# Shifting every stationary operand of the rounded products by 64 bytes, and two small moves in the turn to the output steps

## The chip, the cores and the metric

The kernel runs on one core of one Trainium2 chip. The metric is the device time of one execution in microseconds (us), the median of three runs. The engines are PE (TensorE, with its weight loads listed apart as PEld), DVE (VectorE), ACT (ScalarE), POOL (GpSimd) and SP (SyncE, which here only issues DMAs).

## The reference, cut to what matters

Three networks follow each other: a windowed attention over 4 x 8 heads of 576 positions, a gated product network, and a second network with a SiLU between its two products.

```
attn = softmax(mask(q @ k.T * scale)) @ v      # window of 64 behind each position
x  = attn as 2304 x 512
x  = ((x @ w1) * (x @ w2)) @ w3 @ w_out        # 512 -> 1024 -> 1024 -> 512
h  = x @ w_in                                  # 512 -> 2048
y  = (h * sigmoid(h)) @ w_out2                 # 2048 -> 512
```

All inputs come as 64-bit floats' words, which the kernel converts itself.

## The kernel before, in words

**Rounded products.** Most matmuls take operands that were split into a high part (rounded to the type `fp32r`) and a low part (what the rounding left). A product of two such operands is three matmuls: high by high, high by low, low by high (`PASSES`). Each matmul has a stationary operand (128 x 128, loaded by a weight load of its own) and a moving one, which streams past it: 384 columns in the first two stages, 256 in the last.

**Stages.** `phase_w` converts weights and forms w3 @ w_out (plain products) while the first attention units run. `phase_a(blk, hooks)` runs six times, once for each block of 384 positions: 16 groups `ab` of 12 matmuls (stationary `hl`, the split w1 and w2; moving `xa` and `xb`; L693 and one left-over at L698) and 4 groups `x` of 24 (stationary `wp`, moving `p` and `q`; L723 and L729). Blocks 0 to 4 carry the attention between their groups: `unit` calls `halves_to`, and each `half` puts scores `s`, values `o` and three transposes `t` on PE, and the softmax on DVE and ACT. The transposes (L428) read `sm`, the normalised weights that DVE writes last in a unit (L418). Chunks of w_in are converted in the same units. The last block has no attention. Then come 12 steps `d` of the hidden layer (`h_slot`, `product`, L1019: 7 groups of 12, stationary `wi`, moving the tiles `xop`, which lie in the slots x0 to x6), and 36 output steps `m` (`out_products`, L1170: 42 matmuls of 256 columns, stationary `hi`, `lo` and `a`, moving the weight parts `wo`). Both use a fast matrix scheme of seven products, so there are sums of operands to build.

**Order.** Everything runs under a manual schedule: what stands in the program is the order on each engine, and an engine does its instructions in that order. Ahead of output step m stand, for its operands, `f_load` (a DMA of hidden values), `f_sums` (DVE), `f_high` (ACT casts) and `f_low` (DVE subtractions); for its weights, `o_load` and `o_part` (ACT casts and DVE subtractions for pair n of w_out2; step m with m % 4 = e uses the pairs 2e and 2e + 1). `keep` stores a hidden tile, `read` empties a PSUM bank.

**Where operands lie.** Tiles live in named slots that are used again and again; `SLOTS` gives sizes in 4-byte elements, 1024 where a name is missing. In the program as built, every slot but x0 to x6 begins 128 bytes behind a multiple of 256. The slots x0 to x5 have 1568 elements, that is 6272 bytes or 24.5 times 256, so they begin by turns 128 and 0 bytes behind such a multiple. All operands of rounded products thus begin at a multiple of 128 bytes, except the ones that `shifted` cuts out: `hi` and `lo` in x0 to x5 begin 16 elements, 64 bytes, further. Of the 42 stationary operands of an output step that leaves 36 shifted and 6 (`a`) not; in every fourth step (m % 4 = 3: `lo` in xa, `hi` in x6) all 42 are unshifted. Over 36 steps 972 of 1512 are shifted and 27 x 6 + 9 x 42 = 540 are not.

Of the kernel before, what the change touches and what calls it, by code (L numbers as in the profile page):

```python
# [9 lines left out]
F32 = mybir.dt.float32  # L10
F32R = mybir.dt.float32r
# [31 lines left out]
def tile_window_attention_ffn(ctx, tc, qkv, qkp, vp, w1, w2, w3t, w_out, w_in, w_out2, out):  # L43
# [53 lines left out]
    x2d = dram.tile([4, 128, T], F32, name="x2d", tag="x2d")  # L97
    w_in32 = dram.tile([4, 128, FF2], F32, name="w_in32", tag="w_in32")

    SLOTS = {"p": 4096, "q": 2304, "xa": 1536, "xb": 1536, "xr": 1536, "st": 1024, "x2": 4096, "cv_r": 512, "cv_b": 512}  # L100
    SLOTS.update({"xe": 2304, **{f"x{i}": 1568 if i < 6 else 1536 for i in range(7)}})

    def slot(name, tag, dims, dtype=F32, pool=None, bufs=1):

        t = (pool or main).tile([128, SLOTS.get(tag, 1024)], dtype, name=name, tag=tag, bufs=bufs)
        n = int(np.prod(dims))
        letters = "abcd"[: len(dims)]
        sizes = {x: d for x, d in zip(letters[1:], dims[1:])}
        return t[:, :n].rearrange(f"p ({' '.join(letters)}) -> p {' '.join(letters)}", **sizes)
# [636 lines left out]
                nc.gpsimd.memset(f32(pt[i, 0][hs, 1 - h]), 0.0)  # L746

    with tc.manual_schedule():
        xr = slot("xr", "xr", [4, NB])
        xe = slot("xe", "xe", [2304])  # L750
        phase_w()
# [30 lines left out]
        late.close()  # L782

        end = ctx.enter_context(tc.tile_pool(name="end", bufs=1, side="right"))
        PAIRS = FF2 // 256
        SUPER = T // (2 * NB)
        DUOS = PAIRS // 2
        NDUO = DUOS * SUPER
# [4 lines left out]
        gd = dram.tile([SUPER, DUOS, 128, 4, 768], F32, name="gd", tag="gd")  # L793
        t32 = dram.tile([PAIRS, 128, 7, 256], F32, name="t32", tag="t32")
        xop, raw, wop, oop = {}, {}, {}, {}
        g, bank, tmp = {}, {}, {}
# [8 lines left out]
        def sub(eng, out, a, b):  # L805
            tt(eng, out, a, b, ALU.subtract)
# [13 lines left out]
        shared = {}  # L820

        def unit_tile(kind, n, i):

            tag = UNITS[n // 2][6 if i == 3 else 3 * (n % 2) + i]
            key = kind, tag
            if key not in shared:
                if tag[0] == "p":
                    if (kind, "p") not in shared:
                        shared[kind, "p"] = slot(f"{kind}_p", "p", [4, 1024], F32R)
                    shared[key] = shared[kind, "p"][:, int(tag[1])]  # L830
                else:
                    shared[key] = slot(f"{kind}_{tag}", tag, [1024], F32R)
            return shared[key]
# [95 lines left out]
        def o_load(n):  # L929
            if n in (0, 2, 4):  # L930
                t = [tmp["q"][:, 0:1024], tmp["q"][:, 1024:1536], tmp["q"][:, 1536:1792]]
            elif n == 1:
                t = [xe[:, 0:1024], xe[:, 1024:1536], xe[:, 1536:1792]]
            elif n == 7:
                x = slot("or7", "xb", [1536])
                t = [x[:, 0:1024], x[:, 1024:1536], st[3][:, 768:1024]]
            else:
                t = [st[2], st[3][:, 0:512], st[3][:, 512:768]]
            raw["o", n] = t
            for x, y in zip(t, (slice(0, 4), slice(4, 6), slice(6, 7))):  # L940
                nc.sync.dma_start(out=x, in_=t32[n, :, y].rearrange("p a n -> p (a n)"))
# [13 lines left out]
        def o_part(n, part):  # L955
            if part == 0:
                o_tiles(n)
            r0, r1, r2 = raw["o", n]
            src = [r0[:, 0:512], r0[:, 512:1024], r1, r2]
            src = [x.rearrange("p (a n) -> p a n", n=256) for x in src]  # L960
            for i in ((0, 1), (2,), (3,), ())[part]:
                nc.scalar.copy(out=oop[n][i][0], in_=src[i])
            for i in ((), (0,), (1,), (2, 3))[part]:
                sub(nc.vector, oop[n][i][1], src[i], f32(oop[n][i][0]))
# [43 lines left out]
        def product(d, k):  # L1008
            t, first, i = WHERE[k]
            j, e = divmod(d, DUOS)  # L1010
            x, name = xop[j, i], home(d, k)
            fresh = k in (0, 2, 5)
            if fresh:
                bank[name] = pso.tile([128, 2, 512], F32, name=f"{name}{d}_{k}", tag=name)
            for q in range(2):
                w = wop[2 * e + q][t]
                for kt in range(2):
                    for n, (l, r) in enumerate(PASSES):
                        nc.tensor.matmul(  # L1019
                            bank[name][:, q, 0:NB], lhsT=w[:, l, first + kt], rhs=x[:, kt, r, :],  # L1020
                            start=(fresh and kt == 0 and n == 0), stop=(kt == 1 and n == 2), skip_group_check=True,
                        )
# [7 lines left out]
        def keep(d, op, t):  # L1030
            j, e = divmod(d, DUOS)
            nc.sync.dma_start(out=gd[j, e, :, op], in_=t.rearrange("p t q n -> p (t q n)"))
# [47 lines left out]
        def f_load(m):  # L1080
            if m >= NTG * DUOS:
                return
            if m == 0 or m % 3 == 2:
                t = xe[:, 0:1024], xe[:, 1024:2048]
            elif m > 1 and m % 3 == 1:
                t = slot(f"f{m}", "w21", [1024]), slot(f"fs{m}", "w22", [1024])
            else:
                t = tmp["q"][:, 0:1024], tmp["q"][:, 1024:2048]
            raw["f", m] = t
            tg, e = divmod(m, DUOS)  # L1090
            cols = slice(tg % 3 * 256, tg % 3 * 256 + 256)
            nc.sync.dma_start(out=t[0].rearrange("p (a n) -> p a n", a=4), in_=gd[tg // 3, e, :, :, cols])

        def f_sums(m):

            if m < NTG * DUOS:
                f, t = [x.rearrange("p (a n) -> p a n", a=4) for x in raw["f", m]]
                add(nc.vector, t[:, 0], f[:, 3], f[:, 2])  # L1100
                sub(nc.vector, t[:, 1], f[:, 3], f[:, 0])
                sub(nc.vector, t[:, 2], t[:, 0], f[:, 0])
                sub(nc.vector, t[:, 3], f[:, 1], t[:, 2])

        def shifted(name, tag):

            t = slot(name, tag, [SLOTS[tag]], F32R, end)
            t = t[:, 16:1552] if SLOTS[tag] > 1536 else t
            return t.rearrange("p (a n) -> p a n", a=6)

        def f_high(m):
            if m < NTG * DUOS:
                n = m % 4
                if n == 3:
                    lo = slot(f"lo{m}", "xa", [6, 256], F32R)
                    a = unit_tile("wo", 6, 3)[:, 0:512]
                else:
                    if "a11" not in tmp:
                        tmp["a11"] = slot("a11", "xr", [3, 512], F32R)
                    lo = shifted(f"lo{m}", ("x1", "x5", "x4")[n])  # L1120
                    a = tmp["a11"][:, n]
                hi = shifted(f"hi{m}", ("x0", "x2", "x3", "x6")[n])
                a = [a[:, 0:256], a[:, 256:512]]
                sets[m] = lo, hi, a
                f, t = raw["f", m]
                for i, x in ((0, f), (3, t)):
                    nc.scalar.copy(out=hi[:, i : i + 3], in_=x[:, 0:768].rearrange("p (a n) -> p a n", a=3))  # L1127
                nc.scalar.copy(out=a[0], in_=t[:, 768:1024])

        def f_low(m):  # L1130
            if m < NTG * DUOS:
                lo, hi, a = sets[m]
                f, t = raw["f", m]
                for i, x in ((0, f), (3, t)):
                    sub(nc.vector, lo[:, i : i + 3], x[:, 0:768].rearrange("p (a n) -> p a n", a=3), f32(hi[:, i : i + 3]))
                sub(nc.vector, a[1], t[:, 768:1024], f32(a[0]))
# [121 lines left out]
        for j in range(1, SUPER):  # L1258
# [6 lines left out]
            for k, x in ((14, 3), (16, 4), (18, 6)):  # L1265
                at(s + k, x_op, j, x)
        PLAN = tuple((n, 12 + 5 * n) for n in range(PAIRS))
        FIRST_OUT = 7 * DUOS * (SUPER - 1)
# [20 lines left out]
        xb, xa = slot("gxb", "xb", [2, 768]), slot("gxa", "xa", [2, 768])  # L1289
        st = [slot(f"gst{i}", "st", [1024], bufs=4) for i in range(4)]  # L1290
# [15 lines left out]
        o_part(5, 3)  # L1306
        o_load(6)
        keep(last, 2, g["a22"])
        f_sums(2)
        product(last, 4)  # L1310
        product(last, 6)
        read(last, 4)
        f_sums(3)
        for part in range(4):
            o_part(6, part)
        keep(last, 1, g["a12"])
        o_load(7)
        f_high(2)
        read(last, 6)
        keep(last, 3, g["two", last % 2])  # L1320
        f_low(2)
        f_load(5)
        for part in range(4):
            o_part(7, part)
        f_high(3)
        f_low(3)
        f_load(6)
        f_sums(4)
# [85 lines left out]
```

## Time and profile before

| | |
|---|---|
| median of 3 runs | 822.27 us (822.09 to 823.5) |
| the profiled execution | 821.25 us, of which the span of its instructions is 819.3 us |
| busy in the span | PE 804.2, DVE 633.0, ACT 562.8, POOL 340.2 us |
| stretch 112 to 166 us (blocks 0 and 1) | PE 54.00 of 54.00, DVE 39.37, ACT 44.02 |
| stretch 166 to 397 us (blocks 1 to 4) | PE 230.37 of 231.00, DVE 197.96, ACT 204.58 |
| stretch 460.77 to 642.44 us (hidden steps) | PE 181.21 of 181.67, DMA share 0.74 |
| stretch 642.44 to 819.30 us (output steps) | PE 171.44 of 176.86, DMA share 0.43 |

PE looks busy nearly throughout, but a matmul's own record is longer than the distance to the next one, since they are pipelined. How fast PE goes is read from starts: so many matmuls from one start to another. The profiled execution is 1.02 us under the median.

### The profile page before, as it was taken

The numbers are of one execution on the slowest core, as the hardware profiler recorded it, in microseconds if no ns is written. First come the engines' busy times: TensorE is split into PE (matmuls) and PEld (weight loads), VectorE is DVE, ScalarE is ACT, GpSimd is POOL, SyncE is SP. The second block draws the span as 40 slices with busy tenths as digits, with TensorE's granted clock in tenths as the row PEclk, the third lists the DMA queues.
The fourth block names the chain that finished last, engine by engine and source line by source line (L and its number), as shares of the span: only waits on it lengthen the run. The fifth ranks groups of instructions, "written<-read, shape, count | busy, mean of one in ns | idle before, by whom it ended". The sixth has DMA issues, their size and how long they took to land.

```text
span 819.3 us, 15577 instructions
## 1 busy us (share of the span) xinstructions
PE 804.2 (98%) x5066; PEld 760.5 (93%) x5066; DVE 633.0 (77%) x1549; ACT 562.8 (69%) x1314; POOL 340.2 (42%) x422
## 2 busy tenths in 40 slices
PE   8899999999999999999999999999999999999998
PEld 4455799999999999999999999999999899999998
DVE  7878867788888988988747568858546899988882
ACT  6889878889899888989735567765657654334440
POOL 5768576667677677776733204443000000000000
PEclk9999999999999999999999999999999999999999
DMA  9998323534544544544232449797685745544421
GB/s 301 344 310 269 107 76 116 178 101 147 174 136 160 178 145 135 177 150 135 87 126 77 161 165 321 265 352 294 221 290 179 259 154 156 154 139 146 129 78 52
DMA packets 79791, 146.33 MB, mean 179 GB/s; under 512 B 7136, under 2 KB 46432, under 8 KB 79712
## 3 DMA queue, kind: packets, MB, share of 16 engines
q1 hardware_dynamic: 76112, 140.50, 51.7%
q10 hardware_dynamic: 3600, 4.85, 1.6%
q8 instruction: 40, 0.66, 0.3%
q14 instruction: 39, 0.32, 0.1%
HBM read 105.48 MB, written 39.85 MB: 177 GB/s over the span
## 4 chain that ended last, share of the span: by engine, by line
PE 72%; POOL 6%; ACT 6%; issue 4%; DVE 2%; DMA 2%; SPq 0%; ACTq 0%; POOLq 0%; DVEq 0%
PE ab L693 16%; PE oa L1170 11%; PE x L723 9%; PE ob L1170 8%; PE ha L1019 6%; PE hd L1019 6%; PE hb L1019 5%; PE hc L1019 3%; PE accw L614 2%; POOL klo L351 2%; PE t L428 2%; POOL vhl L369 1%; POOL p L117 1%; POOL xr L474 1%; PE o L462 1%
## 5 line engine op out<-in xcount | busy, mean ns | idle before, releaser
L693 PE MATMUL ab<-xa,hl 128*128 128x384 f32 x576 | 118.9, 341 | 0.0
L693 PE MATMUL ab<-xb,hl 128*128 128x384 f32 x570 | 115.2, 334 | 0.0
L693 PEld LDWEIGHTS ab<-xb,hl 128*128 128x128 f32 x570 | 100.3, 188 | 0.0
L693 PEld LDWEIGHTS ab<-xa,hl 128*128 128x128 f32 x576 | 99.1, 188 | 0.0
L1170 PE MATMUL oa<-wo_w,hi 128*128 128x256 f32 x408 | 74.3, 277 | 0.0
L351 POOL TENSOR_TENSOR klo<-qk,qkhi 64x192 fp32r<-64x192 f32 x110 | 67.2, 611 | 8.4 <-ACT qkhi L345 2.3
L723 PE MATMUL x<-p,wp 128*128 128x384 f32 x360 | 69.0, 339 | 0.0
L474 POOL TENSOR_TENSOR xr<-ot 128x128 f32<-128x128 f32 x55 | 32.7, 595 | 72.8 <-DVE ot L473 56.0
L1170 PEld LDWEIGHTS oa<-wo_w,hi 128*128 128x128 f32 x408 | 61.8, 188 | 0.0
L723 PEld LDWEIGHTS x<-p,wp 128*128 128x128 f32 x360 | 61.8, 188 | 0.0
L1170 PE MATMUL oa<-wo_w,lo 128*128 128x256 f32 x204 | 56.7, 278 | 0.0
L1019 PE MATMUL ha<-xop,wi_w 128*128 128x384 f32 x288 | 54.4, 337 | 0.5 <-ACT gxb L1041 0.5
L1019 PEld LDWEIGHTS ha<-xop,wi_w 128*128 128x128 f32 x288 | 50.5, 188 | 1.1 <-ACT gxb L1041 1.1
L406 ACT ACTIVATE sm<-sm,nm 128x192 f32<-128x192 f32 x110 | 49.3, 449 | 1.4
L887 POOL TENSOR_TENSOR cv_b<-cv_b,cv_r 128x512 int32<-128x512 int32 x16 | 22.3, 1394 | 62.7 <-DVE cv_b L884 50.9
L1019 PE MATMUL hd<-xop,wi_w 128*128 128x384 f32 x252 | 48.0, 336 | 0.0
L345 ACT CAST qkhi<-qk 128x768 fp32r<-128x768 f32 x55 | 46.0, 836 | 1.2
L392 DVE CUSTOM_DVE_ANT_0 sm<-s,consts 128x192 f32<-128x192 f32 x144 | 45.2, 352 | 1.3 <-PE s L385 0.9
L1019 PEld LDWEIGHTS hd<-xop,wi_w 128*128 128x128 f32 x252 | 44.4, 188 | 0.0
L428 PE MATMUL t<-consts,sm 128*128 128x128 f32 x216 | 35.9, 275 | 7.4 <-DVE sm L418 5.3
L1170 PE MATMUL ob<-wo_w,hi 128*128 128x256 f32 x216 | 40.8, 278 | 0.3 <-ACT hi L1127 0.3
L723 PE MATMUL x<-q,wp 128*128 128x384 f32 x210 | 40.3, 334 | 0.0
(279 smaller groups left out, 2261.1 us busy)
## 6 DMA issues: line engine op xcount, KB each, us to landing
qk<-in_qkv SPq DMA_DIRECT2D x55, 384.0 KB, 3.1
words<-in_w3t SPq DMA_DIRECT2D x16, 512.0 KB, 6.5
words<-in_w SPq DMA_DIRECT2D x16, 512.0 KB, 6.2
xe<-in_w_in SPq DMA_DIRECT2D x16, 512.0 KB, 4.6
gq<-in_w_out SPq DMA_DIRECT2D x16, 512.0 KB, 4.9
gd<-gxa SPq DMA_DIRECT2D x18, 384.0 KB, 4.4
gd<-gst SPq DMA_DIRECT2D x18, 384.0 KB, 4.9
xe<-gd SPq DMA_DIRECT2D x13, 512.0 KB, 4.0
```

Of the source, the lines that this page charges most:

```text
L345: nc.scalar.copy(out=hi, in_=t)
L351: nc.gpsimd.tensor_tensor(out=k_lo[g % 2][hs, h * 192 : h * 192 + 192], in0=t[hs, n], in1=f32(hi[hs, n]), op=ALU.subtract)
L392: nc.vector.tensor_tensor_reduce(out=sm[g % 2][:, h, :], in0=s_ps[:, h, :], in1=consts[:, at + 64 - 64 * h : at + 256 - 64 * h], op0=ALU.a ...
L406: nc.scalar.activation(out=e[:, h, :], in_=x, func=AF.Exp, scale=-1.0, bias=nm[:, h : h + 1], accum_out=sums_of[g % 2][:, h, 0:1])
L428: nc.tensor.transpose(t_ps[:, i * 128 : i * 128 + 128], x[:, at : at + 128], id_sb)
L474: nc.gpsimd.tensor_tensor(out=xr[:, c, r : r + 128], in0=t[:, 0:128], in1=t[:, 128:256], op=ALU.add)
L614: nc.tensor.matmul(acc[i], lhsT=w3x[s % 7][:, i * 128 : (i + 1) * 128], rhs=wo[:, j], start=(j == 0), stop=(j == 7))
L693: nc.tensor.matmul(acc, lhsT=w[:, l, fs], rhs=x[k // 2][:, k % 2, r, :], start=(k == 0 and n == 0), stop=(k == 3 and n == 2),)
L723: nc.tensor.matmul(acc, lhsT=wp[f][:, l, o * 128 : (o + 1) * 128], rhs=p[f][:, r, :], start=(f == 0 and n == 0), stop=(f == 7 and n == 2),)
L887: nc.gpsimd.tensor_tensor(out=c.b, in0=c.b, in1=c.r, op=ALU.add)
L1019: nc.tensor.matmul(bank[name][:, q, 0:NB], lhsT=w[:, l, first + kt], rhs=x[:, kt, r, :], start=(fresh and kt == 0 and n == 0), stop=(kt == ...
L1170: nc.tensor.matmul(dst, lhsT=lhs[l], rhs=rhs[r], start=(first and e == 0 and q == 0 and n == 0), stop=(e == DUOS - 1 and q == 1 and n == 2 ...
```

## The change

The sizes of slots and the order in which they are first asked for change, so that slots which hold stationary operands begin 64 bytes behind a multiple of 128; `SKIP` and the argument `skip` move a tile inside its slot by 16 elements. `xa` and the `xop` tiles, which are moving operands, get skips that leave them at a multiple of 128. The moving weight parts `wo` of the output steps share their slots with stationary ones and are shifted with them.

In the program as built, all stationary operands of the lines L693, L698, L723, L729, L1019 and L1170 (two to six lines further down in the new file) begin 64 or 192 bytes behind a multiple of 256. Moving operands of the first five of these lines begin 0 or 128 behind one, as before. Of the 1512 products of the output steps, whose moving operands all began 128 behind one, 1323 now have a moving operand at 192 and 189 one at 64; stationary and moving lie 0 apart modulo 256 in 999 of them and 128 apart in 513. Before, they lay 64 apart (either way) in 972 and 0 apart in 540. In the hidden steps they lay 0 apart in 576 products and 128 apart in 432; now they lie 64 apart, either way, in all 1008. Operands of the attention and of `phase_w` stay where they were modulo 128.

The second part moves steps ahead of the output: `f_high(2)` and `f_low(2)` go ahead of `o_part(6)`, `f_high(3)` too, `o_load(7)` goes up.

```diff
-    SLOTS = {"p": 4096, "q": 2304, "xa": 1536, "xb": 1536, "xr": 1536, "st": 1024, "x2": 4096, "cv_r": 512, "cv_b": 512}
-    SLOTS.update({"xe": 2304, **{f"x{i}": 1568 if i < 6 else 1536 for i in range(7)}})
+    SLOTS = {"p": 4112, "q": 2304, "xa": 1552, "xb": 1536, "xr": 1552, "st": 1024, "x2": 4096, "cv_r": 512, "cv_b": 512}
+    SLOTS.update({"xe": 2304, **{f"x{i}": 1552 for i in range(7)}})
+    SKIP = {"xa": 16, "x6": 16, "x1": 16, "x3": 16, "x5": 16}
...
+        t = t[:, SKIP.get(tag, 0) if skip is None else skip :]
...
     with tc.manual_schedule():
+        for t in ("q", "xb", "p", *[f"w{i}" for i in range(24)], "xa"):
+            slot(f"first_{t}", t, [1])
...
         end = ctx.enter_context(tc.tile_pool(name="end", bufs=1, side="right"))
+        for i in (6, 0, 1, 2, 3, 4, 5):
+            slot(f"first_x{i}", f"x{i}", [1], pool=end)
...
-                        shared[kind, "p"] = slot(f"{kind}_p", "p", [4, 1024], F32R)
+                        shared[kind, "p"] = slot(f"{kind}_p", "p", [4, 1024], F32R, skip=16)
...
         def shifted(name, tag):
 
-            t = slot(name, tag, [SLOTS[tag]], F32R, end)
-            t = t[:, 16:1552] if SLOTS[tag] > 1536 else t
-            return t.rearrange("p (a n) -> p a n", a=6)
+            return slot(name, tag, [6, 256], F32R, None if tag == "xa" else end, skip=16 - SKIP.get(tag, 0))
...
-                    lo = slot(f"lo{m}", "xa", [6, 256], F32R)
+                    lo = shifted(f"lo{m}", "xa")
...
-                        tmp["a11"] = slot("a11", "xr", [3, 512], F32R)
+                        tmp["a11"] = slot("a11", "xr", [3, 512], F32R, skip=16)
...
         keep(last, 2, g["a22"])
+        o_load(7)
         f_sums(2)
+        f_high(2)
         product(last, 4)
         product(last, 6)
         read(last, 4)
         f_sums(3)
-        for part in range(4):
-            o_part(6, part)
+        f_low(2)
+        f_load(5)
         keep(last, 1, g["a12"])
-        o_load(7)
-        f_high(2)
         read(last, 6)
         keep(last, 3, g["two", last % 2])
-        f_low(2)
-        f_load(5)
-        for part in range(4):
-            o_part(7, part)
         f_high(3)
+        for n in (6, 7):
+            for part in range(4):
+                o_part(n, part)
         f_low(3)
```

On DVE, at the turn from the hidden to the output steps, this stood before. `xe` and `gq` are the sums for steps 2 and 3, `wo_w<-gst` is `o_part(6)`, `wo_p<-or` and the row behind it `o_part(7)`, `gxa<-hd` is `read(last, 6)`, `lo<-xe` is `f_low(2)` and `lo<-gq` `f_low(3)`.

```order
L800 TENSOR_TENSOR gq<-gq 128x256 x4
L800 TENSOR_TENSOR wo_w_7839<-gst_6122,wo_w_7839 128x512
L800 TENSOR_TENSOR wo_w_7840<-gst_6122,wo_w_7840 128x512
L800 TENSOR_TENSOR wo_w_7841<-gst_6123,wo_w_7841 128x512
L800 TENSOR_TENSOR wo_w_7702<-gst_6123,wo_w_7702 128x256
L800 TENSOR_TENSOR gxa<-hd_5_7705,gxa 128x768
L800 TENSOR_TENSOR lo_7855<-xe,hi_7856 128x768 x2
L800 TENSOR_TENSOR a_7673<-xe,a_7673 128x256
L800 TENSOR_TENSOR wo_p<-or_7851,wo_p 128x512 x3
```

The same place of DVE in the new program:

```order
L806 TENSOR_TENSOR gq<-gq 128x256 x4
L806 TENSOR_TENSOR lo_7849<-xe,hi_7850 128x768 x2
L806 TENSOR_TENSOR a_7708<-xe,a_7708 128x256
L806 TENSOR_TENSOR gxa<-hd_5_7740,gxa 128x768
L806 TENSOR_TENSOR wo_w_7897<-gst_6157,wo_w_7897 128x512
L806 TENSOR_TENSOR wo_w_7898<-gst_6157,wo_w_7898 128x512
L806 TENSOR_TENSOR wo_w_7899<-gst_6158,wo_w_7899 128x512
L806 TENSOR_TENSOR wo_w_7737<-gst_6158,wo_w_7737 128x256
L806 TENSOR_TENSOR wo_p<-or_7841,wo_p 128x512 x3
```

The low parts for step 2 now stand ahead of `read(last, 6)`, and the four subtractions of `o_part(6)` behind both.

On ACT, the same place before (`gst<-hb` is `read(last, 4)`, `gxa<-gxa` the SiLU of `read(last, 6)`):

```order
L1028 ACTIVATE gst_6120<-hb_0_7609 128x768
L962 CAST wo_w_7839<-gst_6122 128x512
L962 CAST wo_w_7840<-gst_6122 128x512
L962 CAST wo_w_7841<-gst_6123 128x512
L962 CAST wo_w_7702<-gst_6123 128x256
L1127 CAST hi_7856<-xe 128x768 x2
L1128 CAST a_7673<-xe 128x256
L1028 ACTIVATE gxa<-gxa 128x768
L962 CAST wo_p<-or_7851 128x512 x3
L962 CAST wo_p<-gst_6123 128x256
L1127 CAST hi_7877<-gq 128x768 x2
```

And in the new program:

```order
L1131 CAST hi_7850<-xe 128x768 x2
L1132 CAST a_7708<-xe 128x256
L1034 ACTIVATE gst_6155<-hb_0_7644 128x768
L1034 ACTIVATE gxa<-gxa 128x768
L1131 CAST hi_7893<-gq 128x768 x2
L1132 CAST wo_p<-gq 128x256
L968 CAST wo_w_7897<-gst_6157 128x512
L968 CAST wo_w_7898<-gst_6157 128x512
L968 CAST wo_w_7899<-gst_6158 128x512
L968 CAST wo_w_7737<-gst_6158 128x256
L968 CAST wo_p<-or_7841 128x512 x3
```

The casts of `o_part(6)` now stand behind the SiLU `gxa<-gxa`, which needs DVE's `gxa<-hd`, and behind the casts of `f_high(3)`. On SP the load of pair 7 and the load for step 5 moved ahead of the stores of the last hidden tiles; PE and POOL keep their order.

## Rows read from the trace of the kernel before

**Rows 1.** The page: busy time of the engines, and PE's granted clock in 40 slices.

```profile
PE 804.2 (98%) x5066; PEld 760.5 (93%) x5066; DVE 633.0 (77%) x1549; ACT 562.8 (69%) x1314; POOL 340.2 (42%) x422
...
PEclk9999999999999999999999999999999999999999
```

**Rows 2.** Chain that ended last, output steps: start us, us, what (matmuls).

```profile
728.60 2.72 PE oa L1170 x24
...
733.44 2.88 PE oa L1170 x24
```

**Rows 3.** The chain, block 5 of the gated network.

```profile
414.50 29.64 PE ab L693 x171
...
449.33 11.44 PE x L723 x66
```

**Rows 4.** The chain, a hidden step: a group with moving slot x4, one with x1.

```profile
547.70 2.08 PE hb L1019 x12
549.78 2.12 PE ha L1019 x12
```

**Rows 5.** Timeline of PE in block 1, transposes of five units: start us, us, what.

```profile
174.45 0.49 PE L428 MATMUL t<-consts,sm 128*128 128x128 f32 x3
...
195.42 0.49 PE L428 MATMUL t<-consts,sm 128*128 128x128 f32 x3
```

**Rows 6.** Timeline of DVE in block 1, the instructions on which those transposes wait.

```profile
172.31 0.56 DVE L418 TENSOR_TENSOR sm<-sm,rs 128x384 f32<-128x384 f32 x1
...
193.66 0.56 DVE L418 TENSOR_TENSOR sm<-sm,rs 128x384 f32<-128x384 f32 x1
```

**Rows 7.** Timeline of all engines, one attention unit late in block 4.

```profile
379.91 0.56 DVE L418 TENSOR_TENSOR sm<-sm,rs 128x384 f32<-128x384 f32 x1
...
380.61 0.52 PE L428 MATMUL t<-consts,sm 128*128 128x128 f32 x3
380.85 0.42 DVE L472 TENSOR_TENSOR ot<-o,ot 64x256 f32<-64x256 f32 x1 [0.38 <-ACT ot L471]
...
382.69 0.51 ACT L114 CAST q<-a 128x384 fp32r<-128x384 f32 x1 [0.83 <-DVE a L709]
...
384.85 0.48 ACT L707 COPY a<-ab 128x384 f32<-128x384 f32 x1
...
386.19 0.42 DVE L472 TENSOR_TENSOR ot<-o,ot 64x256 f32<-64x256 f32 x1 [0.38 <-ACT ot L471]
```

**Rows 8.** Waits from 140 to 167 us: who for whom, us, times, longest.

```profile
ACT pt L438 <- PE t L428: 1.2, 3, 0.6
```

**Rows 9.** The chain, two places in the hidden steps.

```profile
490.36 2.38 PE ha L1019 x12
...
527.07 4.74 DMA gd<-gxb
```

**Rows 10.** Timeline of all engines at the turn to output step 2.

```profile
645.00 1.97 ACT L962 CAST wo_w<-gst 128x512 fp32r<-128x512 f32 x4 [3.59 <-DMA gst<-t]
645.66 2.23 DVE L800 TENSOR_TENSOR wo_w<-gst,wo_w 128x512 fp32r<-128x512 f32 x4 [3.19 <-ACT wo_w L962]
...
646.88 1.56 ACT L1127 CAST hi<-xe 128x768 fp32r<-128x768 f32 x2
...
647.76 0.50 PE L1170 MATMUL ob<-wo_w,hi 128*128 128x256 f32 x2 [0.33 <-ACT hi L1127]
647.81 0.95 DVE L800 TENSOR_TENSOR gxa<-hd,gxa 128x768 f32<-128x768 f32 x1
648.67 1.82 DVE L800 TENSOR_TENSOR lo<-xe,hi 128x768 fp32r<-128x768 f32 x2
648.79 0.84 ACT L1028 ACTIVATE gxa<-gxa 128x768 f32<-128x768 f32 x1
...
649.68 0.38 PE L1170 MATMUL ob<-wo_w,lo 128*128 128x256 f32 x1 [1.42 <-DVE lo L800]
...
653.21 0.95 DVE L800 TENSOR_TENSOR lo<-gq,hi 128x768 fp32r<-128x768 f32 x1
```

More of the change, by code (lines that the diff above doesn't have):

```diff
@@ L98, in tile_window_attention_ffn, with slot @@
     w_in32 = dram.tile([4, 128, FF2], F32, name="w_in32", tag="w_in32")
-    SLOTS = {"p": 4096, "q": 2304, "xa": 1536, "xb": 1536, "xr": 1536, "st": 1024, "x2": 4096, "cv_r": 512, "cv_b": 512}
-    SLOTS.update({"xe": 2304, **{f"x{i}": 1568 if i < 6 else 1536 for i in range(7)}})
-    def slot(name, tag, dims, dtype=F32, pool=None, bufs=1):
+    SLOTS = {"p": 4112, "q": 2304, "xa": 1552, "xb": 1536, "xr": 1552, "st": 1024, "x2": 4096, "cv_r": 512, "cv_b": 512}
+    SLOTS.update({"xe": 2304, **{f"x{i}": 1552 for i in range(7)}})
+    SKIP = {"xa": 16, "x6": 16, "x1": 16, "x3": 16, "x5": 16}
+    def slot(name, tag, dims, dtype=F32, pool=None, bufs=1, skip=None):
         t = (pool or main).tile([128, SLOTS.get(tag, 1024)], dtype, name=name, tag=tag, bufs=bufs)
         n = int(np.prod(dims))
+        t = t[:, SKIP.get(tag, 0) if skip is None else skip :]
         letters = "abcd"[: len(dims)]
```

## Prediction

> **What bounds the kernel now.** I read the page first: PE is busy for 98% of the span at the full clock, 2.4 GHz, in every slice [rows 1]. But overlapping records hide the question, so I took the distance from one matmul's start to the next from the chain.
>
> In the output steps 24 matmuls of 256 columns take 2.72 us where the stationary operands are shifted, 113.3 ns each, and 2.88 us, 120.0 ns each, in a step where none is [rows 2]. The columns alone are 256 / 2.4 = 106.7 ns, so 6.7 or 13.3 ns come on top. With 384 columns and nothing shifted, 171 matmuls take 29.64 us and 66 take 11.44: 173.3 ns, which is 160 and again 13.3 [rows 3]. The extra is the same at both lengths, so I expect a shifted operand to save the same 6.7 ns at 384 columns.
>
> A second reading: in the hidden steps a group of 12 takes 2.08 us with the moving slot x4 and 2.12 with x1, that is 3.3 ns more per matmul, with stationary operands that lie alike [rows 4]. What differs is where the moving operand lies: modulo 256 at the same place as the stationary one, or 128 bytes away. So the price is not the stationary address's alone; the place of the two to each other counts.
>
> Then I asked where PE is the bound. In block 1 the transposes come every 5.24 us (20.97 over four) and the DVE instruction that feeds them every 5.34 (21.35 over four); its result is ready 1.58 us early at 174.45 and 1.20 at 195.42 [rows 5, 6]. DVE falls back by 0.1 us per unit, although PE does not hold it. Late in block 4 the reserve is gone: the result is ready at 380.47 and the transposes start 0.14 later [rows 7]. The same rows show why DVE goes at 5.34: a ring without PE. DVE's L472 to L709 run back to back, ACT's L114 waits for L709, ACT then works through to L707 and the copies behind it, and for these the next L472 waits: 380.85 to 386.19. From about 166 to 397 us the attention is paced by this ring.
>
> **The change part by part.** The sum is against the profiled execution's 821.25 us; the runs' median is 1.02 above.
>
> A, blocks 0 and 1 up to 166 us. Some 250 rounded products, 6.7 ns each: 1.7 us at most. ACT and DVE still wait for PE here, ACT 1.2 us for transposes [rows 8], so a faster PE moves the ring forward by about that. Bounds 0 and -1.7; I take **-1.2**, the wait that the row shows.
>
> From there to 397 us: 0. The 1,000 or so products get faster, and PE waits at each transposition instead, by 5.34 less 5.08 us a unit (24 x 6.7 ns off 5.24) [rows 5, 6].
>
> B, 397 to 460.8 us, the last 73 products of block 4 and the 288 of block 5, without a ring: 361 x 6.7 = **-2.4**. Bound 0, if 384 columns gain nothing.
>
> C, hidden steps: 1008 x 6.7 = -6.7; where the moving slot lies 128 away, 432 products also lose their 3.3 ns, -1.4, if a distance of 64 frees them of it. I count half, -0.7. Against that stand waits that PE's speed uncovers: the group at 490.36 already takes 2.38 us instead of 2.12, for ACT, and the store of gxb, 4.74 us, sits on the chain ahead of another [rows 9]. DMAs and ACT do not get faster, so I add 0.9 for these two and their kind (each grows by 0.3 us over the four groups between). **-6.5**, bounds -8.1 and -4 (and 0 without a gain at 384 columns).
>
> D, output steps. Two prices are possible, and this is the largest uncertain term. If only the stationary address counts, the 540 unshifted products fall from 120.0 to 113.3 ns [rows 2]: -3.6. If the place to each other counts, the shared slots undo the gain: stationary and moving are now both shifted, 0 or 128 apart, and no product is 64 apart any more. The 972 that were go from 113.3 to 120.0: +6.5; and 513 lie 128 apart and pay up to 3.3 more [rows 4], +1.7, of which I count half. No row shows a shifted moving operand. I take the second, **+7.4**, because x1 against x4 shows the relation at work; the bounds are -3.6 and +8.2.
>
> E, the turn. Step 2 waits 0.33 us for its casts and 1.42 for its low parts, because DVE does `o_part(6)` first, after idling 3.19 us for it [rows 10]. The move fills that idle time: low parts from 642.5 to 644.7 (1.82, and some 0.35 for `a`), then `read(last, 6)` to 645.5. Both waits go. But ACT's casts for pair 6 now stand behind the SiLU, which follows that DVE sum (0.84, to 646.4), and behind the casts for step 3 (1.56 and some 0.3, to 648.3); then come 1.97 for pair 6 and as much for pair 7, to 652.2. DVE's subtractions end 0.9 behind a set of casts, as they did before, at 653.1, and only then come step 3's low parts: 653.21 before, so all but unchanged, the first half at 654.05. Step 3 needs them at its third matmul. So what is late next is step 3, which starts about 653.9 instead of 654.7: **-0.8**. Bounds 0 and -1.75. SP's moved load for pair 7 is hidden: it was not waited for longer than pair 6's casts last.
>
> Shifting tiles inside slots costs the other engines nothing that a row shows, and the empty first allocations issue nothing.
>
> Sum: -1.2 - 2.4 - 6.5 + 7.4 - 0.8 = -3.5, so 817.75 on the profiled execution's scale, **818.8 us** at the median.
>
> The Trainium skill, in "TensorE: Matmul & The Clock Gate" (sections "Wait — 56ns, not 53.3ns?" and "Step-by-step: what each phase is for"), speaks against any gain: starts are N / 2.4 plus about 2.5 ns apart, and weight loads have a read port of their own and take nothing from a running matmul. By that, 256 columns would cost 109.2 ns wherever operands lie, and the sum would be E alone. This trace disagrees: 113.3 and 120.0.
>
> **The rivals.**
> - *Both addresses count* (above): 818.8, by itself 816 to 821.2. Chance 0.48.
> - *The stationary address alone counts.* For it: both the shifted forms in the output steps cost the same, and the moving ones all lay alike there. Against: x1 and x4. D is -3.6: 821.25 - 14.5 + 1.02 = 807.8, between 805 and 811. Chance 0.27.
> - *Slower.* The extra at 384 columns has another origin than at 256 (there the load has 53 ns more to hide in), A to C are nothing, and D turns to +7.4: 821.25 + 6.6 + 1.02 = 828.9. It decides from a gain under 6.6 us / 1619 products (A to C) = 4.1 ns each. Against it: the same 13.3 at both lengths. Chance 0.11.
> - *No address effect*, as by the cited rule: the shifts do nothing, E remains, 821.5. Against: 120.0 beside 113.3. Chance 0.05.
> - *The attention follows PE.* If the ring had play that the rows don't show, some 1,000 more products count, 7 us: 811.8 with the first case. Against: PE waits already. Chance 0.04.
> - The rest, 0.05: no gain at 384 columns but one in the output steps, 817.9, or waits in the hidden steps that eat C.
>
> **How the numbers follow.** Between 805 and 822 lie nearly all of the first two cases and the last three; the slow one is left out: 0.8. A measurement tells from no change what is beyond 0.2%, 820.6 to 823.9. Faster: 0.41 of the first case, 0.27, 0.04 and 0.04 of the rest, 0.76. Same: 0.06 of the first, 0.05 of the fourth, 0.11. Slower: the third and what is left of the first and the rest, 0.13.
>
> **What would show it.** In the profile after: twelve matmuls of 384 columns in 2.00 us instead of 2.08, with no difference between slots, if the gain carries over. In the output steps 24 matmuls in 2.88 us throughout by the first case, 2.72 throughout by the second. Transposes in blocks 1 to 4 still 5.34 us apart, with PE waiting for L418. Step 2 without a wait, step 3 with about a microsecond of it. The prediction fails by 11 us if shifted moving operands cost nothing, and by 10 the other way if 384 columns gain nothing.

## The result and the profile after

The changed kernel takes 831.33 us (median of 4 runs, 830.93 to 832.43), the kernel before 822.18 in the same measurement: ratio 1.0117, 95% interval 1.01 to 1.0134. It is 9.1 us slower. The forecast was 818.8, with a range from 805 to 822.

The page of the changed kernel: busy times, and PE's granted clock in 40 slices (against [rows 1]).

```profile
PE 811.7 (98%) x5066; PEld 768.5 (93%) x5066; DVE 633.6 (76%) x1549; ACT 561.9 (68%) x1314; POOL 340.5 (41%) x422
...
PEclk9999999999999999999999999999999899999999
```

One slice is no longer at full clock, the 33rd, around 660 us. That is the turn.

The chain that ended last in the changed kernel, at the places of [rows 2 to 4] and at the turn: start, length, what.

```profile
415.41 24.70 PE ab L695 x142
...
450.39 10.65 PE x L725 x61
...
546.86 2.08 PE ha L1025 x12
...
551.02 2.10 PE ha L1025 x12
...
650.05 7.46 DMA gd<-gxa
657.51 0.02 issue
657.54 0.97 DVE lo L806
658.51 0.04 issue
658.55 1.22 PE ob L1174 x4
...
691.19 2.85 PE oa L1174 x24
```

With 384 columns nothing was gained: 24.70 / 142 = 173.9 ns and 10.65 / 61 = 174.6, where [rows 3] gave 173.3. Twelve hidden products take 2.08 and 2.10 us, not 2.00. In the output steps 24 products take 2.85 us, 118.8 ns each, where [rows 2] had 2.72 and 2.88. And the output is reached through the landing of a store, of which [rows 10] show nothing.

Both programs issue the same 5066 matmuls in the same order, so their starts can be compared one by one. The changed kernel is behind by 0.6 us when block 0 ends, by 0.7 at the end of block 4, 1.1 at the end of block 5, 1.05 at the end of the hidden steps (642.44 us in the kernel before). Over the next 120 matmuls it loses 4.5 us, and over the remaining output steps 4.6, to 10.2 at the last matmul. The two profiled executions differ by 831.18 - 821.25 = 9.9 us.

The timeline of the changed kernel, PE and DVE in block 1 (as [rows 5, 6]), then DVE, ACT, SP's queue and PE at the turn (as [rows 10]); in brackets what the engine waited for.

```profile
169.81 0.49 PE L430 MATMUL t<-consts,sm 128*128 128x128 f32 x3
...
190.85 0.49 PE L430 MATMUL t<-consts,sm 128*128 128x128 f32 x3
...
167.25 0.56 DVE L420 TENSOR_TENSOR sm<-sm,rs 128x384 f32<-128x384 f32 x1
...
188.89 0.56 DVE L420 TENSOR_TENSOR sm<-sm,rs 128x384 f32<-128x384 f32 x1
...
643.27 1.82 DVE L806 TENSOR_TENSOR lo<-xe,hi 128x768 fp32r<-128x768 f32 x2
...
646.33 0.85 ACT L1034 ACTIVATE gxa<-gxa 128x768 f32<-128x768 f32 x1 [3.02 <-DVE gxa L806]
...
648.78 0.52 SPq L1098 DMA_DIRECT2D xe<-gd  x1
649.40 0.56 SPq L1038 DMA_DIRECT2D gd<-gst  x1
650.05 0.38 SPq L1038 DMA_DIRECT2D gd<-gxa  x1
...
657.54 1.83 DVE L806 TENSOR_TENSOR lo<-gq,hi 128x768 fp32r<-128x768 f32 x2 [3.02 <-DMA gd<-gxa]
...
658.55 0.58 PE L1174 MATMUL ob<-wo_w,lo 128*128 128x256 f32 x1 [4.66 <-DVE lo L806]
```

Transposes come every 5.26 us and DVE's L420 every 5.41 (21.04 and 21.64 over four; the same four units of the kernel before took 20.97 and 21.55): the attention runs as before. At the turn the low parts of step 2 are early now (643.27), but those of step 3 start at 657.54 instead of 653.21. Their tile takes the place of `gxa`, and `gxa` is still being stored. The store is issued at 650.05, 1.27 us behind the load of set 5 (`xe<-gd`, 512 KB), and lands 7.5 us after its issue. Its data itself goes late: the last two stores, this one and the one of `gst` issued at 649.40, are the only transfers here with packets of 3 KB, and of their 256 packets the first starts at 652.90 and the last ends at 657.14, 0.4 us before the landing. PE waits 4.66 us. What that costs beyond the wait is in the windows of the changed kernel: stretch, its length, busy time and instructions of each engine, granted clock, DMA share, GB/s.

```profile
650.00:655.00 5.00, 3.89 (x33) 3.68 (x31) 3.96 (x8) 3.61 (x7) 0.00 (x0) 1.00 0.92 298
655.00:660.00 5.00, 1.45 (x7) 1.45 (x8) 2.46 (x5) 0.00 (x0) 0.00 (x0) 0.59 0.16 62
660.00:665.00 5.00, 5.00 (x33) 5.00 (x33) 4.93 (x13) 3.65 (x6) 0.00 (x0) 0.73 0.36 107
665.00:670.00 5.00, 5.00 (x44) 5.00 (x43) 4.93 (x12) 2.97 (x5) 0.00 (x0) 1.00 0.59 176
```

While the store waits for its turn the DMA engines are busy (0.92 of the time from 650 to 655 us). After PE's wait the clock stands at its lower level, 1.2 GHz, for a while (granted 0.73 from 660 to 665 us): 33 matmuls start in 5 us instead of 44. By their starts 18 matmuls were 100 ns late each, 1.8 us.

### The profile page after: what moved, and what is told of

The parts are those of the page before. It is cut to its first block, busy times and chain, and to the rows that moved or that the text cites. A ratio compares the mean times of both kernels' runs of the same rounds, so it can differ in the third digit from the quotient of the medians.

```text
span 829.4 us, 15574 instructions
## 1 busy us (share of the span) xinstructions
PE 811.7 (98%) x5066; PEld 768.5 (93%) x5066; DVE 633.6 (76%) x1549; ACT 561.9 (68%) x1314; POOL 340.5 (41%) x422
## 4 chain that ended last, share of the span: by engine, by line
PE 73%; ACT 8%; POOL 5%; issue 3%; DVE 3%; DMA 2%; ACTq 0%; SPq 0%; POOLq 0%; DVEq 0%
PE ab L695 17%; PE oa L1174 11%; PE x L725 9%; PE ob L1174 8%; PE ha L1025 6%; PE hd L1025 5%; PE hb L1025 5%; PE hc L1025 3%; PE accw L616 3%; PE t L430 2%; POOL klo L353 2%; PE o L464 1%; POOL vhl L371 1%; DMA gd<-gxa 1%; PE s L383 1%
## 5 line engine op out<-in xcount | busy, mean ns | idle before, releaser
L695 PE MATMUL ab<-xa,hl 128*128 128x384 f32 x576 | 118.8, 342 | 0.0
L1174 PE MATMUL oa<-wo_w,hi 128*128 128x256 f32 x408 | 77.6, 285 | 0.0
L1174 PEld LDWEIGHTS oa<-wo_w,hi 128*128 128x128 f32 x408 | 63.8, 192 | 0.0
```

The source lines that it names most:

```text
L695: nc.tensor.matmul(acc, lhsT=w[:, l, fs], rhs=x[k // 2][:, k % 2, r, :], start=(k == 0 and n == 0), stop=(k == 3 and n == 2),)
L1174: nc.tensor.matmul(dst, lhsT=lhs[l], rhs=rhs[r], start=(first and e == 0 and q == 0 and n == 0), stop=(e == DUOS - 1 and q == 1 and n == 2 ...
```

## The experiments

My theory after the result: (1) the place of the two operands to each other sets the price at both lengths, and at 384 columns a distance of 64 gains nothing; (2) the turn loses by its new order, through the late store. The rivals: the stationary address alone counts and something else in the kernel hides its gain; the turn loses because products or buffers are slower.

**The address by itself.** A kernel of matmuls only, executed once: three to a triple as in the products here, 42 for each pair of offsets, stationary and moving tiles both beginning 128 behind a multiple of 256.

```diff
+        def combo(a, b, cols, count):
...
+                for n, (l, r) in enumerate(((0, 0), (0, 1), (1, 0))):
+                    c = 256 * (i % 12) + 128 * l + a // 4
+                    m = cols * (2 * (i % 4) + r) + b // 4
```

> This kernel computes nothing of the reference: only TensorE works, on triples of products as the kernel has them (one stationary address twice, then another; two moving addresses), 42 for each pair of offsets. With 256 columns, if the place of the two operands to each other sets the price: 113.3 ns from start to start where they lie 64 bytes apart modulo 128, 120.0 ns where they lie 0 apart. If the stationary address alone sets it: 113.3 in every cell whose stationary operand is shifted, 120.0 in the others. If neither counts: one number everywhere. With 384 columns the changed kernel showed 173 to 176 ns with the stationary operand shifted, about as before: if the 6.7 ns cannot be had at this length, all cells are near 173; if it was hidden there by something else in the kernel (other engines' accesses), some cells show 167.

Mean distance from start to start in ns, from the trace; rows are the stationary operand's offset in bytes, columns the moving one's. The first six products of each cell are left out, since the distance still changes there (in the cell +0, +192: 116, 120, 114, 123, 119, then 113 to 114):

```
256 columns   +0     +64    +128   +192      384 columns   +0     +64    +128   +192
st +0        119.9  117.7  118.7  113.3                   173.6  173.3  176.0  176.7
st +64       117.8  120.0  117.8  118.7                   176.7  173.3  173.3  176.0
st +128      118.7  113.3  119.9  117.8                   176.0  176.6  173.3  173.3
st +192      117.8  118.7  113.3  119.8                   173.3  176.0  176.7  173.3
```

The chain of this kernel in four stretches, stationary at +0: 256 columns with moving at +0 and +192, then 384 columns with +64 and +192.

```profile
63.94 4.07 PE acc L68 x34
...
78.89 4.21 PE acc L68 x37
...
189.97 6.59 PE acc L68 x38
...
204.47 6.54 PE acc L68 x37
```

The first two read as 119.7 and 113.8 ns, the others as 173.4 and 176.8 (a stretch has some of a cell's first products in it, and its last matmul is cut by its edge, so up to half a ns off). No row and no column of the table is even: the place to each other counts, modulo 256. With 384 columns it is a clean rule: 173.3 (173.6 in the first cell) where the moving operand lies at the same place or 64 ahead, 176.0 at 128, 176.7 at 192 ahead. Nothing goes below 173.3, also not with offsets of 16, 32, 48 and 96 bytes of either operand against the other at +0. So at none of the places tried do the 6.7 ns exist at this length. With 256 columns 0 apart is the dearest of these places, 120. A moving operand 64 ahead cost 117.7 or 117.8 in all four cells, one 64 behind (192 ahead) 113.3 in three and 117.8 in one. The rule is one of multiples of 64 only: 16 ahead also gave 113.3 at 256 columns, but 175.5 at 384.

**Where 64 apart is cheap.** The same, with the third product's stationary address at an offset of its own, each pair once behind another pair and once behind 12 products that lie 0 apart.

```diff
-                    c = 256 * (i % 12) + 128 * l + a // 4
+                    c = 256 * (i % 12) + 128 * l + (a2 if l and a2 is not None else a) // 4
```

> Again TensorE alone, and nothing of the reference: 256 columns, with offsets of their own for the stationary address that is used twice and for the one behind it. In the first grid a moving operand 64 bytes ahead of the stationary one (modulo 256) cost 113.3 ns in three cells of four, and one 64 bytes behind 117.8 in all four, while the kernel before had 113.3 to 113.9 in both directions, with its two stationary operands 128 apart. If the alternation makes 113.3: cells whose two stationary operands are 128 apart and both 64 from the moving one are near 113.3 at either turn, with or without 12 unshifted products ahead. If what ran ahead decides: the two turns differ. All cells where the two operands coincide stay at 120.

The expectation has the two sides of the first grid the wrong way round: the three cheap cells of four have the moving operand 64 behind, not ahead. One execution gave this, again without the products in which the distance still changes:

```
all 64 from the moving operand; ns, first turn / second turn
high part 64 ahead of the moving operand, low part 64 behind     113.3 / 113.3    114.1 / 113.5
high part 64 behind, low part 64 ahead                           118.9 / 113.4    113.3 / 118.9
both 64 ahead                                                    117.8 / 117.8    117.8 / 113.4
both 64 behind                                                   117.8 / 113.4    117.8 / 117.8
both at the same place as the moving operand                     119.9 / 120.1    120.0 / 119.6
```

Each line has two placements. Both answers of the expectation are partly right: with the two stationary operands on either side of the moving one, high part ahead, it was 113 to 114 in all four tries. The other pairings at 64 were seen in two states, 113.3 and 117.8 to 118.9; between the two turns of a cell only the products ahead, the length of the sequence and the PSUM bank differ, and the cell with both 64 behind that went from 117.8 to 113.4 wrote the same bank in both turns. So what ran ahead decides which state they stay in.

**Shifts without the new turn.** The steps from `last = NDUO - 1` to the loop of output steps as they stand in the kernel before.

```diff
-        f_high(2)
         product(last, 4)
...
+        for part in range(4):
+            o_part(6, part)
         keep(last, 1, g["a12"])
+        o_load(7)
+        f_high(2)
         read(last, 6)
```

> The changed kernel with the order of before at the turn, so the addresses alone. The matmuls' starts of the two kernels moved apart by 4.5 us at the turn and by 4.7 us over the output steps. If the turn's loss comes from the order alone: 831.3 - 4.5 = 826.8 us, and the output steps still at 119 ns a product. If it comes from the addresses (slower products, later buffers): about 831, with a wait of 4 us or more left at the turn.

826.47 us, ratio 1.0048 (1.003 to 1.0066) to the kernel before, which ran at 823.3 in this measurement. Its wait at the turn (who for whom, us, times, longest), and an output step of its chain:

```profile
PE ob L1174 <- DVE lo L806: 1.4, 1, 1.4
...
691.43 2.86 PE oa L1174 x24
```

PE's wait at the turn is 1.4 us, with full clock, and the output steps are at 119.3 ns on average. So the order makes the loss at the turn, and the addresses make the other.

**The new turn without shifts.** The other way round.

> The kernel before with the new order at the turn, so the order alone. If the order makes the loss: 822.2 + 4.5 = 826.7 us, one wait of nearly 5 us of TensorE for the low parts of step 3, and the output steps at 113.3 and 120.0 as before. If the order is worth what was forecast: 821.4 us.

827.13 us, ratio 1.0051 (1.0036 to 1.0066). Its waits from 600 to 720 us (who for whom, us, times, longest), and a window of it:

```profile
PE ob L1170 <- DVE lo L800: 5.5, 1, 5.5
```

```profile
660.00:665.00 5.00, 5.00 (x27) 5.00 (x27) 4.93 (x13) 3.61 (x6) 0.00 (x0) 0.56 0.37 105
```

The wait and the fall of the clock are the order's own. Ratios of 1.0048 and 1.0051 add up to 1.0099; the change measured 1.0117 (1.01 to 1.0134). Each of the three has an interval of 0.0015 to 0.0018 to either side, so the two parts account for the whole as far as these times can tell.

**The load behind the stores.**

```diff
         f_low(2)
-        f_load(5)
         keep(last, 1, g["a12"])
         read(last, 6)
         keep(last, 3, g["two", last % 2])
+        f_load(5)
```

> The changed kernel with the load of set 5 (512 KB) issued behind the last two stores of the hidden steps in SP's queue; nothing else moves. In the changed kernel the store of gxa, whose place the low parts of step 3 take, was issued 0.65 us behind that load and landed 7.5 us later. If the load in front of it makes it late: it lands in 3 to 4 us, step 3 waits about 1 us, and the time falls by about 4 to 827.3 us. If it is late for its input (the SiLU) or for the other traffic: 831.3 as before.

829.76 us, ratio 1.0082 (1.0068 to 1.0097): 1.6 us better by the medians and 2.9 by the ratios, since the kernel before ran at 823.3 here; not the 4 expected. The chain of this kernel, and PE's wait:

```profile
649.01 6.62 DMA gd<-gxa
...
PE ob L1174 <- DVE lo L806: 2.7, 1, 2.7
```

The store is issued a microsecond earlier and still takes 6.6 us. PE's wait falls from 4.7 to 2.7 us. The load, which had stood 1.27 us ahead of this store (the 0.65 of the expectation is the distance to the store of `gst`), was part of it; in front of the store there are still the loads of pair 7 and the store of `gst`, which went out at 641.44 in the kernel before, and here only 0.5 us ahead, behind those loads.

**All stores first.** In the kernel before: low parts of step 2 early as in the change, the store of `gxa` ahead of the loads of pair 7 and set 5, and step 3's low parts taking turns with pair 7's (`casts` and `subs` are the two halves of `o_part`).

```diff
         f_sums(2)
+        f_high(2)
...
+        f_low(2)
         keep(last, 1, g["a12"])
-        o_load(7)
-        f_high(2)
+        casts(6, (0, 1))
         read(last, 6)
         keep(last, 3, g["two", last % 2])
-        f_low(2)
+        o_load(7)
         f_load(5)
-        for part in range(4):
-            o_part(7, part)
+        casts(6, (2, 3))
+        subs(6, (0, 1, 2, 3))
         f_high(3)
...
```

> The kernel before with another order at the turn: low parts of step 2 ahead of pair 6 as in the change, but the store of gxa is issued ahead of the loads of pair 7 and of set 5, and the low parts of step 3 and pair 7's subtractions alternate. If the late store was what made the changed order lose: TensorE waits at step 3 for 0.5 to 1.5 us and nowhere else, where the kernel before waited 2.1 at step 2, the granted clock stays full, and the time is 820.6 to 821.7 us. If loads and stores together fill the queues whatever their order: a wait of 3 us or more, with a fall of the clock, 824 us or more.

822.55 us, ratio 1.0007 (0.9998 to 1.0017): no change that could be told. Its timeline, and a line of its chain:

```profile
647.41 0.32 SPq L1032 DMA_DIRECT2D gd<-gxa  x1
...
650.53 0.96 DVE L800 TENSOR_TENSOR lo<-gq,hi 128x768 fp32r<-128x768 f32 x1 [1.58 <-DMA gd<-gxa]
653.77 0.69 DVE L800 TENSOR_TENSOR wo_p<-or,wo_p 128x512 fp32r<-128x512 f32 x1 [2.27 <-ACT wo_p L1307]
...
647.82 5.27 DMA or<-t
```

The store now lands in time for 650.53, 3.0 us after its issue at 647.41. But the load of pair 7 behind it takes 5.3 us, where it took 3.3 in the kernel before, and DVE waits for that: step 3 waits 1.6 us in three pieces. The clock stays full. The moved order costs nothing once the store goes first, and gains nothing either.

**Output operands back.** In `shifts_old_turn`, only the stationary tiles of the output steps go back to multiples of 128; the moving ones stay shifted.

```diff
-            return slot(name, tag, [6, 256], F32R, None if tag == "xa" else end, skip=16 - SKIP.get(tag, 0))
+            return slot(name, tag, [6, 256], F32R, None if tag == "xa" else end)
...
-                        tmp["a11"] = slot("a11", "xr", [3, 512], F32R, skip=16)
+                        tmp["a11"] = slot("a11", "xr", [3, 512], F32R)
```

> The kernel of shifts_old_turn (826.5 us) with one thing undone: the stationary operands of the output steps lie on multiples of 128 again, the moving ones stay shifted by 64. By the place of the two to each other they are again 64 apart, so 113.3 to 118 ns a product instead of 119.3: 1512 products give 2 to 9 us back, 817.5 to 824.5 us. By the stationary address alone all of them are unshifted now and cost 120: 827 us or more.

819.72 us, ratio 0.9978 (0.9968 to 0.9988), from 1.0048: 0.7% or 5.8 us for moving the stationary operands to where the stationary-address theory calls them bad. The chain of this kernel:

```profile
691.47 2.72 PE oa L1174 x24
```

113.3 ns in this step. Over all 1512 output products it is 114.5, with the dearer ones in the steps m % 4 = 0 (116 ns). The stationary address alone is refuted.

**All operands at one place.** In the kernel before, all x slots, `xa` and `a11` at 192 modulo 256, weights and `wo` at 128.

```diff
-    SLOTS.update({"xe": 2304, **{f"x{i}": 1568 if i < 6 else 1536 for i in range(7)}})
+    SLOTS.update({"xe": 2304, **{f"x{i}": 1536 for i in range(7)}})
...
+        if tag == "xa" or name == "a11":
+            t = t[:, 16:]
...
```

> The kernel before, its turn untouched, weights and moving w_out operands where they were (128 modulo 256), but every x slot, the low parts of each fourth output step and the tile a11 at 192 modulo 256. By the grid: the hidden steps' products are all 64 ahead, 173.3 ns, where 430 cost 176.1 (-1.2 us); output products are 64 behind: 113.3 as in the kernel before for 1458 of 1512 (before 972), which is -3.2 us, 822.2 - 4.4 = 817.8 us; or 117.8 as in the grid, +4.3 - 1.1 = +3.2 for them, 824.2 us. If addresses don't matter: 822.2.

823.58 us, ratio 1.0024 (1.0013 to 1.0035), near the dearer of the two cases. (That case took 117.8 from the wrong side of the first grid: the moving operand is 64 behind here, where the grid had 113.3 in three cells and 117.8 in one. That it came near is luck.) The chain of this kernel:

```profile
551.88 2.08 PE hd L1021 x12
...
693.80 2.83 PE oa L1170 x24
```

The hidden steps have 173.3 ns in every slot now, as the grid says. The 1458 output products, both parts 64 ahead of the moving operand, average 117.1 ns: both states of the second grid, more of the dear one. A distance of 64 alone is not enough.

**A version by these rules.** In the kernel before: weights, `wo`, `xa` and `xb` at 192 modulo 256, x slots 64 ahead of the weights in the hidden steps, high parts at 0 and low parts at 128, that is on either side of `wo`, high part ahead. (The expectation's "64 ahead of... the moving operand" is said of the high parts.)

```diff
-    SLOTS.update({"xe": 2304, **{f"x{i}": 1568 if i < 6 else 1536 for i in range(7)}})
+    SLOTS.update({"xe": 2304, **{f"x{i}": 1568 if i in (1, 4, 5) else 1536 for i in range(7)}})
+    SKIP = {"x4": 32}
+    SKIP_OUT = {"x1": 32, "x5": 32, "xa": 48}
...
+            return slot(name, tag, [6, 256], F32R, None if tag == "xa" else end, skip=SKIP_OUT.get(tag, 0))
...
```

> The kernel before with its turn and with other places: moving w_out operands and all weights at 192 modulo 256, x slots of the hidden steps 64 ahead of the weights (173.3 ns in the first grid), the high parts of all output steps 64 ahead of... the moving operand, that is at 0, and the low parts at 128, the pairing that gave 113.3 to 113.5 ns in the second grid whatever ran ahead in three of four tries and in the kernel before throughout. Only the 162 products of a11 (128 for both parts) and 54 of w_out's own tile are not so placed. By the place to each other: 270 output products go from 120.0 to 113.5 (-1.8 us), a11's 162 gain 0 to 1, the 430 hidden products of the odd slots gain 2.7 ns (-1.2, less what waits there): 818 to 820 us beside 822. If the stationary address alone counts, all output products lie on multiples of 64 that are multiples of 128, so 120: 822 + 6 = 828 us.

818.76 us, ratio 0.9963 (0.9951 to 0.9976): faster than both kernels. The chain and one window of it:

```profile
552.27 2.08 PE hd L1024 x12
...
690.91 2.72 PE oa L1173 x24
...
693.63 2.04 PE ob L1173 x18
```

```profile
650.00:655.00 5.00, 4.73 (x26) 4.68 (x27) 4.50 (x9) 3.95 (x9) 0.00 (x0) 0.66 0.86 292
```

All kinds of output products but the 54 of `wo`'s own tile average 113.3 to 113.8 ns, those of `a11` too; left out is step 2, part of which ran at the lower clock. The kernel still waits at the turn, and there its clock falls for a while (granted 0.66), which the kernel before did not suffer in its profiled execution.

**Does PE pace the attention?** Products left out of the kernel before.

```diff
+                    if 1 <= blk <= 4 and o and f < 7 and n == 2:
+                        continue
```

> The kernel before with 84 products left out (the hi-by-lo pass of three x2 accumulations in each of blocks 1 to 4, all but the last of each); the result is less exact by that. TensorE has 84 x 173 ns = 14.6 us less to do between 166 and 397 us. If the ring of DVE and ACT paces the attention there, as forecast: 0 to -1 us, TensorE waits at the transposes instead, blocks still 63.9 us long. If TensorE paces it: up to -14.6 us, 808 us, blocks 60.2 us.

819.49 us, ratio 0.9964 (0.9952 to 0.9976): 2.6 us for 14.6 us of products. DVE's timeline in this kernel, against [rows 6, 7]:

```profile
193.25 0.56 DVE L418 TENSOR_TENSOR sm<-sm,rs 128x384 f32<-128x384 f32 x1
...
379.32 0.56 DVE L418 TENSOR_TENSOR sm<-sm,rs 128x384 f32<-128x384 f32 x1
```

186.07 us from one to the other, 186.25 in the kernel before: 0.2 us. Most of the rest comes when the ring ends: the last transposes of block 4 start at 399.97 instead of 401.69, since PE has no products left over there. By the starts this kernel is 3.6 us ahead when block 5 ends, 0.4 of which it has from the beginning; at the turn its clock falls too, and 1.2 us are lost again.

## Why the prediction was wrong

Two terms failed, and each alone would have turned the sign of the forecast.

**What bounds the kernel: "The extra is the same at both lengths, so I expect a shifted operand to save the same 6.7 ns at 384 columns."** This step failed, and with it A, B and C, -10.1 us of the sum. It took an equal remainder (13.3 ns over the columns' time, [rows 2, 3]) for an equal cause. The grid has 173.3 as the floor at 384 columns for every place tried, and the kernel before was already on it, but for the odd x slots. What makes up the 13.3 ns at this length no run shows. Measured by the starts: A +0.6, 166 to 397 us +0.1, B +0.5, C -0.1. The gain that C put down for slots 128 away is real (176.1 ns to 173.4 where the moving operand now lies 64 ahead), but 432 products lie 192 ahead now and take 174.7 (the grid has 176.7 for this place; the difference stayed open). On average the hidden products go from 174.6 to 173.9 ns, -0.7 us, and the waits in two places, grown from 1.0 to 1.5 us, take most of it back. In the gated network the products of `xa` are at 173.0, those of `xb` at 175.2, those of `p` and `q` at 175.6, where all had about 173.6: by the slot sizes `xa` now begins 64 ahead of its weights, the others 192 ahead. Up to 397 us the ring hides that too; behind it, it is B's +0.5. This was the rival *Slower*, at 828.9, to which I gave 0.11. The result is 2.4 us above it, and that it is so near is partly luck: D was 2.8 us too high in it and E 5.3 too low.

**E, the turn: "what is late next is step 3, which starts about 653.9 instead of 654.7".** Step 3 it was, but at 658.55. I followed the DVE instructions in front of its low parts and not the tile that they write: it takes the place of `gxa`, so its first writer waits until the store of `gxa` has landed. Of the DMAs moved in SP's queue I looked only at who waits for pair 7's load, not at what stands behind the loads. -0.8 became +4.5: by the starts a wait of 4.8 us for the 2.1 of before, and 1.8 us for matmuls at the lower clock. The Trainium skill has a rule for such a store, in "DMA: Bandwidth & Descriptors" (section "Queues, rings and completion order"): a DMA's semaphore is counted up by a write that lands only after every earlier write of that DMA engine. The runs do not contradict it but do not show it at work either, since the store's own data was late and the landing followed 0.4 us behind it. What they show is the dependence on what stands in front: the same 384 KB landed 2.8 us after the issue in the kernel before (its issue is the line below; its 128 packets ran from 650.66 to 652.15), 3.0 with the store first, 6.6 and 7.5 with loads and another store in front.

```profile
649.66 0.32 SPq L1032 DMA_DIRECT2D gd<-gxa  x1
```

**D, the output steps: +7.4.** The mechanism was right: the place to each other counts, and sharing slots undid the gain. `out_stationary_back` shows it. The size was off: 972 products went from 113.8 to 119.1 ns, +5.1 for the +6.5 put down, 540 from 119.9 to 119.7, -0.1. A distance of 128 costs nothing on top of 0 at this length (118.7 beside 120), so the +0.8 for that falls away. The starts give +4.6 from 665 us on, behind the first steps.

**The ring in the attention: 0.** Right, and shown by `fewer_products`.

**The rule against any gain.** The price moves with the places by 6.7 ns at 256 columns and by 3.4 at 384, with TensorE alone. The rule of the Trainium skill that I weighed, "TensorE: Matmul & The Clock Gate" (section "Wait — 56ns, not 53.3ns?"), gives 109.2 ns at 256 columns as an estimate; no cell of the grid has it, the lowest is 113.3, and the measurement decides. Why two addresses interact, and why one pair has two lasting states, no run shows: whether weight loads and moving reads meet at one place of SBUF was not tried, and the trace has no record of it.

The sum as measured is 0.6 + 0.1 + 0.5 - 0.1 + 4.5 + 4.6 = 10.2 us, against 9.9 between the profiled executions. Of A's 0.6, 0.3 is there at 80 us, ahead of the first shifted product; kernels with an unchanged beginning differ there by 0.2 to 0.4 either way.

## What to carry to other kernels

A remainder that is equal in two shapes is not the same remainder: before a gain seen at one length is booked for 1600 products of another, look for a row at that length, or time the two lengths alone in a grid of offsets, which takes one small kernel. When stationary and moving tiles share slots, shifting one shifts the other; write down the pair of addresses for each kind of product. When steps are moved, list for each tile that they write who still reads its place, stores included, and for each store what now stands ahead of it in its queue.

## What was not expected of the hardware

With 256 columns and operands 64 bytes apart, one and the same sequence ran at 113.3 or at 117.8 ns per product for dozens of products, depending on what ran ahead (second grid). In the kernel before this shows too: step 2, behind PE's wait, ran at 118 to 119 ns where later steps with the same addresses had 113.3; in `turn_alone` step 2 had 113 to 114.

The granted clock fell to its lower level behind a wait of PE in `turn_alone` (5.5 us), in the changed kernel (4.7 us) and with the load moved (2.7 us). It fell also behind 1.4 us in `out_stationary_back`, in `alternating_places` and in `fewer_products`, but not behind 1.4 us in the kernel before, in `shifts_old_turn` and in `x_slots_at_192`. What tells these apart stayed open. In the profiled executions where it fell at the turn, 12 to 23 matmuls started about 100 ns late each, 1.2 to 2.3 us in all, so the totals of the variants compare places and orders only to about this much; the distances from start to start outside that stretch do not have this error.
